# A new order for every step from the middle of the first feed-forward block on

## The chip, the cores and the metric

The kernel runs on one core of a Trainium2 chip. TensorE (PE in the profile) multiplies matrices, VectorE (DVE), ScalarE (ACT) and GpSimd (POOL) do the element-wise work, and SyncE (SP) issues the DMA transfers. Each engine works through its own list of instructions in the order in which the program wrote them, and waits on semaphores for the others. The metric is the device time of one execution in microseconds (us); a comparison uses the median over several executions.

## The reference

A Mamba-2 state-space layer on 4 batches of 8 heads, 768 positions, head width 32, state width 16, in chunks of 32, is followed by RMS norm and a SwiGLU feed-forward block. All is float32.

```python
for c in range(nc):                      # 24 chunks of 32 positions
    cum = np.cumsum(la, axis=-1)
    L = np.exp(cum[..., :, None] - cum[..., None, :]) * causal
    M = np.einsum('bhin,bhjn->bhij', Cc, Bc) * L
    y[:, :, sl] = np.einsum('bhij,bhjd->bhid', M, xc) + \
                  np.einsum('bhin,bhnd->bhid', Cc, state) * np.exp(cum)[..., None]
    state = decay_full * state + np.sum(Bx, axis=2)
# y is then read as (3072, 256)
xn = x / np.sqrt(np.mean(x * x, axis=-1, keepdims=True) + 1e-06) * rms_g
g = xn @ w_gate                          # (3072, 1536)
return (g * sigmoid(g) * (xn @ w_val)) @ w_out
```

## The kernel before

The 3072 tokens are worked in six blocks of 512. While TensorE multiplies for the feed-forward part of one block, the state-space layer of the next is prepared on the other engines.

**Gate and value.** Each block's two products with the 256 x 1536 weights are made by a Strassen-Winograd scheme: for each of six pairs `j` of 128-column groups, seven products `P.k.j` (`product_gv`, L951) stand for eight. Each is four matmul records of 128x256. Products 1, 4, 6 and 7 add up in a PSUM tile "gate", 2, 3 and 5 in a tile "val"; each of these two has two buffers. Step `take.k.j` copies a "gate" sum to SBUF as `p` (ScalarE, L957), `C.c.j` adds it to the "val" sum (VectorE, L963), `silu.c.j` is ScalarE's activation (L208), and `hid.c.j` (VectorE, `hidp` on GpSimd, L976) multiplies it with the value half into `hid`.

**Output.** Block 0 multiplies `hid` with `w_out` plainly (`o.f`, L983, eight records of 128x256 each). Blocks 1 to 5 use a 3x3 scheme with 20 products: `O.k.h` (`product_o`, L1072, four records of 128x128 for a half `h`), whose factors are sums of pieces of `hid` (`u.n` on VectorE and `up.n` on GpSimd, L1046) and sums of pieces of `w_out` (`two.n`, `twop.n`, L1028). `w.n` adds a product to the output tile `ob` (VectorE, L1103, or ScalarE, L1099 and L208), and `put.i` sends `ob` out (L1108). Ten of the products have no PSUM place of their own and reuse that of an earlier one (the table `SECOND`), so that such a product waits until the earlier one's last `w.n` has been done.

**State-space part and norm.** `spread` (L500, DMA), `sub` (L506) and `ex` (L208, L493) make the decay matrices `L`; `ex` needs another activation table on ScalarE than `silu`, and a table load stands before each change. `T`, `g` (L599), `L1` and `L` (L632), `y` (L736) and `S` (L688) follow. For the norm, `sq` squares, `ms` is a small matmul (L820), `rs` takes the roots on ScalarE and sends them to DRAM (L833), `rb` reads them back to all partitions (L838), `xn` scales (L847), and `tx` (L928) makes the differences that products 4 to 7 need.

**Weights.** In block 0 the weights arrive as raw integers (`fetch`) and are decoded by `pow` (ScalarE, two activations), `man` (VectorE, L224) and `wt` (VectorE, L230).

What sets the order is one string, `order` (from L1269), of 1667 steps. A loop (L1437) calls the function behind each name, block 0's from `first_kinds`, the others' from `kinds`, and each engine's own list is in the order of these calls. A name is block:kind.numbers, so `1:P.4.0` is product 4 of pair 0 in block 1.

Of the kernel before, what the change touches and what calls it, by code (L numbers as in the profile page):

```python
# [20 lines left out]
def kernel(  # L21
# [1217 lines left out]
    def of_chunk(n, fn):  # L1239
# [66 lines left out]
        1:P.2.1 1:C.11.1 0:man.16 1:P.6.1 1:take.6.1 1:P.5.0 1:P.6.0 1:take.6.0 1:P.7.1 1:P.5.1
        0:cwp.1.3 1:silu.11.1 0:wt.16 0:hidgp.22.5 0:sub.11 1:take.7.1 1:C.22.1 1:hid.11.1 0:ydone.3
        0:ex.9 1:P.7.0 0:man.17 1:take.7.0 1:P.4.1 1:P.3.1 1:P.4.0 1:C.22.0 1:silu.21.0 0:wt.17
        1:silu.22.1 1:silu.21.1 0:table.0 1:silu.22.0 1:hidp.22.0 1:dT.1 1:hid.21.0 1:P.3.0 1:cw.2.1
        1:spread.2 1:dT.0 0:o.6 1:spread.3 1:hid.21.1 1:twop.2 1:C.12.1 1:silu.11.0 1:two.3 1:P.1.3  # L1310
        1:take.1.3 1:cwp.2.2 1:hid.11.0 1:P.1.2 1:C.12.0 1:P.2.3 1:P.6.3 1:two.8 0:silug.12.4
        1:silu.12.1 1:hidp.12.1 1:take.1.2 0:hidg.12.4 1:take.6.3 1:sub.3 0:ex.10 1:P.6.2 1:two.0
        0:sq2.2.0.0 0:sq2.2.0.2 1:C.11.3 1:P.2.2 0:sq2.2.1.2 1:twop.1 1:twop.4 1:take.6.2 1:C.11.2
        1:P.7.3 0:sq2.2.1.3 0:ex.11 1:two.11 1:take.7.3 0:sq2.2.1.1 1:T.0.1 0:o.7 0:o.8 1:P.5.3
        1:ex.3 1:hidp.22.1 1:silu.12.0 0:sub.8 1:P.4.3 1:silu.21.3 1:silu.11.3 1:T.1.1 1:hid.12.0
        0:ex.8 1:P.7.2 1:two.5 1:two.10 1:hid.11.3 1:cwp.2.3 0:sq2.2.0.1 1:C.22.3 0:o.9 0:o.10
        0:o.11 1:P.5.2 1:P.3.3 1:silu.22.3 0:sq2.2.0.3 1:bc.0 1:scale2.0 1:take.7.2 1:Tt.0.1
        1:sq2.1.0 1:hid.21.3 1:subp.2 1:twop.7 1:spread.1 1:T.1.0 1:silu.11.2 1:Tt.0.0 1:bc.1
        1:P.4.2 1:silu.21.2 1:C.22.2 1:C.12.3 1:hidp.22.3 1:silu.12.3 1:hidp.12.3 1:x.0 1:subp.1
        1:hid.21.2 1:P.1.4 1:take.1.4 1:P.2.4 1:C.11.4 1:T.0.0 2:bc.0 1:P.3.2 1:Tt.1.1 1:P.6.4  # L1320
        2:bc.1 1:C.12.2 1:P.1.5 1:Tt.1.0 0:put.0 0:put.3 1:hid.11.2 1:P.2.5 1:Td.1 0:put.2
        1:take.6.4 0:put.1 1:take.1.5 1:C.11.5 1:silu.11.5 1:silu.12.2 1:scale2.1 1:hid.12.2 1:P.7.4
        1:P.6.5 1:take.7.4 1:silu.11.4 1:P.5.4 1:take.6.5 2:dT.0 1:P.4.4 1:silu.21.4 1:twop.6
        1:two.9 1:sq2.1.1 1:C.22.4 1:hid.11.5 1:sq2.0.0 1:g 1:hid.11.4 1:silu.22.4 1:Td.0 1:P.7.5
        1:hid.21.4 1:P.5.5 1:silu.22.2 1:L 1:sq2.1.2 1:O.2.0 1:L1.3 1:take.7.5 1:hidp.22.4 1:P.4.5
        1:C.22.5 1:L1.2 1:O.2.1 1:O.15.0 1:O.15.1 1:silu.22.5 1:u.0 1:hid.22.5 1:y.0 1:hid.22.2
        1:silu.21.5 1:w.0 1:hid.21.5 1:u.1 1:P.3.5 1:u.2 1:w.2 1:O.3.0 1:O.3.1 1:O.0.0 1:O.0.1 1:w.4
        1:P.3.4 1:O.17.0 1:C.12.5 1:silu.12.5 1:O.17.1 1:w.5 2:S.0 2:scale2.0 1:hid.12.5 1:w.10
        1:up.3 1:u.9 1:sq2.0.3 1:C.12.4 1:O.6.0 1:silu.12.4 1:O.6.1 0:exps 1:O.16.0 1:O.16.1
        1:sq2.1.3 1:w.1 2:T.1.1 2:Tt.1.1 1:x.1 1:up.4 1:up.5 1:hid.12.4 1:O.4.0 1:up.6 1:u.7  # L1330
        2:Tt.1.0 1:O.4.1 1:O.9.0 1:O.9.1 1:u.10 1:w.3 1:w.6 1:up.11 1:y.1 2:T.0.1 2:Tt.0.0 2:S.1
        1:O.18.0 1:O.18.1 1:sq 1:sq2.0.2 1:yt 1:O.8.0 1:w.11 1:u.8 1:w.12 1:sq2.0.1 1:w.8 1:O.8.1
        1:O.13.0 1:O.13.1 1:w.16 1:ms 1:rs 1:w.13 2:T.1.0 1:O.11.0 1:O.11.1 1:w.7 1:up.12 2:T.0.0
        3:bc.1 1:ex.1 1:O.5.0 1:O.5.1 1:w.20 1:O.12.0 1:O.12.1 2:Tt.0.1 1:O.7.0 1:O.7.1 1:up.13
        1:u.14 2:g 1:w.18 1:O.1.0 1:w.9 1:w.17 1:ex.2 1:O.1.1 1:w.15 1:w.14 1:O.14.0 1:O.14.1 2:Td.0
        1:u.15 1:O.19.0 1:O.19.1 1:w.22 1:w.19 1:rb 1:O.10.0 1:O.10.1 2:scale2.1 1:xn 1:w.24 1:tx.0
        1:txp.1 1:put.3 2:P.1.1 2:take.1.1 1:txp.2 2:spread.2 1:w.25 1:w.21 2:sq2.1.0 2:P.1.0
        1:sub.0 2:take.1.0 1:ex.0 2:P.2.1 2:C.11.1 2:silu.11.1 2:P.6.1 2:P.6.0 2:take.6.0 1:w.23
        2:P.5.1 2:L1.2 2:P.2.0 2:C.11.0 2:take.6.1 2:P.7.0 1:tx.3 2:take.7.0 2:P.7.1 2:take.7.1
        2:P.5.0 2:C.22.1 2:C.22.0 2:silu.22.1 2:P.4.0 2:silu.21.0 2:silu.11.0 2:P.4.1 2:spread.3  # L1340
        2:silu.21.1 2:silu.22.0 2:hid.11.1 2:P.3.1 2:L 2:P.3.0 2:hid.21.0 2:P.1.3 2:hidp.22.0
        2:hid.21.1 2:C.12.0 2:P.1.2 2:silu.12.0 2:hid.12.0 2:take.1.3 2:take.1.2 2:P.2.2 2:C.11.2
        1:put.0 2:L1.3 2:subp.3 2:P.6.3 2:dT.1 2:C.12.1 2:spread.1 2:silu.11.2 2:x.0 2:hid.11.2
        1:put.2 2:ex.3 2:P.6.2 2:take.6.2 3:dT.1 2:Td.1 2:take.6.3 2:hid.11.0 2:sq2.0.0 2:y.0
        2:P.2.3 2:C.11.3 2:sq2.1.2 2:silu.11.3 2:P.7.2 3:scale2.1 2:P.7.3 2:take.7.3 2:take.7.2
        2:subp.2 2:sub.1 2:silu.12.1 2:hidp.12.1 3:S.0 2:sq2.1.1 2:P.5.3 2:C.22.3 2:hid.22.1 2:x.1
        2:silu.22.3 2:hidp.22.3 2:P.5.2 2:C.22.2 2:sq2.1.3 2:P.4.3 2:y.1 3:S.1 2:sq 2:P.4.2
        2:silu.21.2 2:P.3.3 2:hid.21.2 2:C.12.3 2:silu.21.3 2:hid.21.3 2:hid.11.3 2:silu.12.3
        2:P.3.2 1:put.1 2:P.1.5 2:take.1.5 2:silu.22.2 3:T.1.1 3:Tt.1.1 2:C.12.2 2:hidp.12.3
        2:silu.12.2 2:P.1.4 2:sq2.0.3 2:hid.22.2 3:T.0.1 2:take.1.4 2:P.2.5 2:C.11.5 2:silu.11.5  # L1350
        2:hid.11.5 3:spread.0 3:Tt.0.0 2:P.6.5 2:take.6.5 2:P.6.4 2:take.6.4 2:P.2.4 2:C.11.4
        2:P.7.5 2:take.7.5 3:dT.0 2:P.7.4 2:spread.0 2:subp.0 3:Tt.1.0 3:Td.1 2:take.7.4 2:sq2.0.1
        2:P.5.4 2:C.22.4 2:silu.11.4 2:yt 2:silu.22.4 3:subp.0 3:spread.3 2:P.4.5 2:P.4.4
        2:silu.21.4 2:P.5.5 2:ms 2:hid.11.4 2:hid.21.4 2:hidp.12.2 2:O.2.0 2:hidp.22.4 2:up.0
        2:O.2.1 2:O.15.0 2:silu.21.5 2:hid.21.5 2:C.22.5 2:O.15.1 3:exps 2:P.3.5 2:sq2.0.2
        3:spread.2 2:up.1 2:exps 2:u.3 2:up.4 2:rs 2:rb 3:T.1.0 3:T.0.0 2:ex.1 2:w.0 2:P.3.4 2:w.2
        2:O.3.0 2:C.12.5 2:C.12.4 3:sq2.1.0 2:silu.22.5 3:sq2.1.3 2:O.3.1 2:O.0.0 2:silu.12.5
        3:Tt.0.1 2:hid.12.5 2:O.6.0 2:O.6.1 2:O.16.0 2:O.16.1 2:w.1 2:hid.22.5 2:up.5 2:table
        2:O.0.1 3:spread.1 2:silu.12.4 3:g 2:w.4 2:u.2 2:xn 2:O.17.0 2:w.3 2:O.17.1 2:w.5 2:w.10
        3:P.1.0 3:P.2.0 2:hidp.12.4 2:u.9 2:txp.0 2:ex.0 2:tx.2 2:O.4.0 3:take.1.0 2:up.6 2:up.7  # L1360
        2:O.4.1 2:O.9.0 2:O.9.1 2:tx.1 2:tx.3 3:P.6.0 3:take.6.0 3:C.11.0 2:w.6 2:O.18.0 2:O.18.1
        2:w.11 2:w.12 2:w.7 2:w.13 3:P.5.0 2:w.8 2:w.9 2:ex.2 2:u.10 3:P.7.0 2:O.8.0 2:O.8.1
        2:O.13.0 2:O.13.1 2:w.16 3:P.1.1 2:O.5.0 2:O.5.1 3:take.7.0 3:C.22.0 3:silu.22.0 3:P.3.0
        2:up.8 3:take.1.1 3:P.6.1 3:take.6.1 3:P.4.0 3:silu.21.0 3:C.12.0 2:w.20 2:O.7.0 3:L1.3
        3:L1.2 3:sq2.1.2 2:up.11 2:up.12 3:subp.2 2:O.7.1 3:sub.3 3:sq2.0.0 3:silu.12.0 2:O.11.0
        2:O.11.1 3:sq2.0.1 2:O.12.0 2:up.13 2:O.12.1 2:w.17 2:w.15 3:P.7.1 3:take.7.1 2:w.18 2:w.14
        3:hid.21.0 2:u.14 3:table 2:O.1.0 2:O.1.1 2:w.22 3:silu.11.0 2:up.15 2:O.14.0 2:O.14.1
        2:O.19.0 2:O.19.1 3:P.4.1 3:silu.21.1 3:sq2.1.1 2:w.19 2:O.10.0 2:O.10.1 3:hid.22.0 2:w.23
        2:w.24 2:w.25 3:P.1.3 3:P.2.1 3:take.1.3 2:w.21 4:dT.0 3:Td.0 3:C.11.1 3:hid.21.1 3:x.0
        3:bc.0 3:P.2.3 3:subp.1 3:silu.11.1 2:put.3 3:scale2p.0 3:P.6.3 3:hid.12.0 3:hid.11.1  # L1370
# [108 lines left out]
```

## Time and profile before

| | |
|---|---|
| runs | 388.96, 389.95, 391.85 us; median 389.95 us |
| profiled execution | 389.76 us, of which the span from first to last instruction is 388.0 us |
| PE busy | 382.5 us, 99% of the span, 3805 records |
| DVE busy | 277.8 us, 72% |
| ACT busy | 214.3 us, 55%, with 22 table loads |
| POOL busy | 150.1 us, 39% |
| granted TensorE clock | 1.000 |

The profiled execution lies 0.19 us under the median. 1.76 us of it are outside the span. The span is what the views of the trace divide. Busy shares of matmuls overlap in their ends, so that how close TensorE stands to its pace is read from the time between starts, not from the busy time.

### The profile page before, as it was taken

What the parts mean: (1) busy time and instruction counts of PE and PEld (TensorE: products, weight loads), DVE (VectorE), ACT (ScalarE), POOL (GpSimd) and SP (SyncE); (2) the same over time, 40 slices, a digit from 0 to 9 for tenths busy, and PEclk for the clock granted to TensorE, in tenths of its full rate; (3) what the DMA queues carried; (4) which work ended last, traced back from release to release, by engine and by line L of the source; (5) the groups of instructions that cost most, each with busy time, mean ns of one, the idle gap of its engine ahead of it and who ended that gap; (6) DMA issues with size and microseconds to landing.
All of it is one profiled execution on the core that took longest, in us unless ns stands there. A gap on an engine that the chain in (4) does not pass through costs nothing.

```text
span 388.0 us, 9604 instructions
## 1 busy us (share of the span) xinstructions
PE 382.5 (99%) x3805; PEld 330.0 (85%) x3805; DVE 277.8 (72%) x593; ACT 214.3 (55%) x453; POOL 150.1 (39%) x168
## 2 busy tenths in 40 slices
...
PEclk9999999999999999999999999999999999999999
...
GB/s 91 236 128 233 311 169 179 124 166 30 3 101 87 52 11 96 144 42 100 65 75 85 27 42 42 2 18 19 56 3 2 2 14 48 29 1 0 2 0 56
DMA packets 109940, 28.04 MB, mean 72 GB/s; under 512 B 94824, under 2 KB 107848, under 8 KB 109896
## 3 DMA queue, kind: packets, MB, share of 16 engines
...
q14 instruction: 14, 0.11, 0.1%
...
## 4 chain that ended last, share of the span: by engine, by line
PE 97%; DVE 1%; ACT 1%; issue 0%; ACTq 0%; DVEq 0%
PE gate L951 29%; PE o L1072 23%; PE val L951 22%; PE o L983 5%; PE gate L865 4%; PE y L736 3%; PE gate L875 2%; PE g L599 2%; PE e L460 1%; PE g L592 1%; PE y L664 1%; PE tp L540 1%; PE e L474 0%; DVE ob L1103 0%; PE idle L328 0%
## 5 line engine op out<-in xcount | busy, mean ns | idle before, releaser
L963 DVE TENSOR_TENSOR c<-val,p 128x512 f32<-128x512 f32 x99 | 67.3, 686 | 49.4 <-PE val L951 35.2
L957 ACT COPY p<-gate 128x512 f32<-128x512 f32 x99 | 56.8, 581 | 61.6 <-PE gate L951 59.3
L951 PE MATMUL gate<-tx,wgv 128*128 128x256 f32 x264 | 65.8, 381 | 0.0
L208 ACT ACTIVATE c<-c 128x256 f32<-128x256 f32 x99 | 40.0, 415 | 39.2 <-DVE c L963 38.9
L976 POOL TENSOR_TENSOR hid<-c 128x256 f32<-128x256 f32 x31 | 23.8, 769 | 89.6 <-ACT c L208 84.9
L951 PEld LDWEIGHTS gate<-tx,wgv 128*128 128x128 f32 x264 | 49.3, 190 | 6.9 <-ACT p L957 0.2
L1103 DVE TENSOR_TENSOR ob<-ob,o 128x128 f32<-128x128 f32 (+1 forms) x90 | 24.2, 297 | 21.7 <-PE o L1072 16.9
L976 DVE TENSOR_TENSOR hid<-c 128x256 f32<-128x256 f32 x68 | 34.0, 513 | 6.7 <-ACT c L208 6.6
L1072 PE MATMUL o<-two,hid 128*128 128x128 f32 x280 | 36.5, 276 | 0.1
L1072 PEld LDWEIGHTS o<-two,hid 128*128 128x128 f32 x280 | 34.5, 192 | 1.1 <-DVE hid L976 0.4
L951 PE MATMUL val<-xn,wgv 128*128 128x256 f32 x132 | 33.7, 381 | 0.0
L951 PE MATMUL val<-tx,sw 128*128 128x256 f32 x132 | 33.5, 380 | 0.0
L951 PE MATMUL val<-xn,sw 128*128 128x256 f32 x132 | 33.3, 381 | 0.0
L951 PE MATMUL gate<-tx,sw 128*128 128x256 f32 x132 | 33.0, 380 | 0.0
L951 PE MATMUL gate<-xn,wgv 128*128 128x256 f32 x132 | 32.7, 380 | 0.0
L493 POOL TENSOR_SCALAR_AFFINE_SELECT L<-L 64x512 f32<-64x512 f32 x32 | 22.8, 713 | 18.1 <-ACT L L208 16.8
L951 PEld LDWEIGHTS val<-xn,wgv 128*128 128x128 f32 x132 | 24.8, 190 | 3.5
L951 PEld LDWEIGHTS val<-tx,sw 128*128 128x128 f32 x132 | 24.9, 190 | 3.4 <-issue 0.2
L951 PEld LDWEIGHTS gate<-tx,sw 128*128 128x128 f32 x132 | 24.8, 190 | 3.4 <-issue 0.2
L951 PEld LDWEIGHTS val<-xn,sw 128*128 128x128 f32 x132 | 24.4, 190 | 3.2 <-issue 0.2
L951 PEld LDWEIGHTS gate<-xn,wgv 128*128 128x128 f32 x132 | 24.4, 190 | 3.1
L208 ACT ACTIVATE u<-gate 128x256 f32<-128x256 f32 (+1 forms) x37 | 14.6, 402 | 18.2 <-PE gate L951 15.3
(202 smaller groups left out, 702.6 us busy)
## 6 DMA issues: line engine op xcount, KB each, us to landing
...
```

The source lines that it names most:

```text
L208: nc.scalar.activation(**operands)
L493: nc.gpsimd.affine_select(out=L[r], in_=L[r], pattern=[[0, L.shape[1]], [1, HC]], compare_op=ALU.is_ge, fill=0.0, base=0, channel_multipli ...
L599: nc.tensor.matmul(out=g[u, P * i:P * i + P].rearrange("p (t m) -> p t m", t=2), lhsT=T[r, i, 0, u], rhs=T[r, i, 1:3, u], start=(first and ...
L736: nc.tensor.matmul(out=y[2 * k + u][rows, (2 * n + i) * HC:(2 * n + i + 1) * HC], start=(k, u, rows.start) not in opened, stop=True, skip_ ...
L865: nc.tensor.matmul(out=gv[:, k], lhsT=w[:, t, fs], rhs=xns[0][:, t], start=(t == 0), stop=(t == 1))
L951: nc.tensor.matmul(out=dst[:, half[w]], lhsT=lhsT, rhs=rhs, start=(k in (1, 2, 5) and w == 0), stop=True, skip_group_check=True)
L957: nc.scalar.copy(out=t, in_=Xs[j])
L963: nc.vector.tensor_tensor(out=t, in0=Zs[j], in1=a, op=ALU.add)
L976: engine.tensor_tensor(out=hid[:, 2 * j + c // 10 - 1, c % 10 - 1], in0=u, in1=src[:, half[1]], op=ALU.mult)
L983: nc.tensor.matmul(out=o, lhsT=hid[:, f, k // 2, (k % 2) * P:(k % 2 + 1) * P], rhs=wo[:, f], start=opens, stop=(f == NF - 1), skip_group_c ...
L1072: nc.tensor.matmul(out=Os[blk, b][:, place * P:(place + 1) * P], lhsT=hidden_or_sum(u)[:, g], rhs=rhs, start=(blk, b) not in opened, stop= ...
L1103: nc.vector.tensor_tensor(out=o, in0=o, in1=src, op=ALU.add if what[0] == "+" else ALU.subtract)
```

## The change

Every step of the string after `0:P.3.5`, the third product of pair 5 in block 0, stands in a new order: 1333 of the 1667 steps, all but the first behind that product. The set of steps is the same. Each engine has as many instructions as before, except that ScalarE has 20 table loads and not 22, and that the waits between engines differ in number (TensorE 78 before and 74 now, VectorE 188 and 182, ScalarE 96 and 103, GpSimd 69 and 57, SyncE 72 and 78). The order is one that was fitted with a little time added to every hand-over between two engines. Since the first `put` of block 0 is now number 1, the allocation of its output tile asks whether the tile is there, and not for number 0.

```diff
     def put(k):
-        if k == 0:
+        if 0 not in obs:
             obs[0] = ffn.tile([P, 2, 2, DM], FP32, tag="ob", name="ob", bufs=1)
...
-        0:cw.1.1 0:o.2 0:o.3 0:silug.21.5 0:hidg.21.5 1:spread.0 0:cwp.5.3 0:P.3.5 0:pow.14 0:man.14
-        0:wt.14 0:o.4 0:rb.1 0:pow.15 0:sq2.2.1.0 0:fetch.16 0:hidg.11.5 0:pow.17 0:C.12.5 0:C.12.4
...
+        0:cw.1.1 0:o.2 0:o.3 0:silug.21.5 0:hidg.21.5 1:spread.0 0:cwp.5.3 0:P.3.5 0:pow.14
+        0:silug.22.5 0:pow.15 0:cwp.1.3 0:C.12.4 0:silug.12.4 0:pow.17 0:rb.1 1:dT.0 0:sq2.2.1.3
...
-        5:up.13 5:w.14 5:w.9 5:O.12.1 5:w.17 5:w.18 5:w.15 5:put.3 5:u.14 5:O.1.0 5:O.1.1 5:w.19
...
+        5:w.20 5:w.15 5:w.14 5:w.16 5:O.12.0 5:O.12.1 5:O.11.0 5:O.11.1 5:u.14 5:w.22 5:w.18 5:O.5.0
+        5:O.14.0 5:O.5.1 5:w.17 5:put.3 5:u.15 5:O.1.0 5:O.1.1 5:w.19 5:O.19.0 5:O.14.1 5:O.19.1
...
```

**First place: VectorE ahead of block 1's first product.** These rows of VectorE start at the last product of block 0's pair 5, `hid<-u,gate`. `m` and `wo` are the decoding of `w_out`, `c` the sums `C`, `xn` the scaled input of block 1, which its first product on TensorE waits for, and `L<-L,tok` is `0:sub.11`. Before:

```order
L976 TENSOR_TENSOR hid<-u,gate 128x256
L224 TENSOR_SCALAR m<-wr 128x512
L230 TENSOR_TENSOR wo<-m,e 128x512
L976 TENSOR_TENSOR hid<-c 128x256
L963 TENSOR_TENSOR c<-val,p 128x512 x2
L847 SCALAR_TENSOR_TENSOR xn<-yt,gcol,sq 128x512 x2
L928 TENSOR_TENSOR tx<-xn 128x256 x2
```

Now:

```order
L976 TENSOR_TENSOR hid<-u,gate 128x256
L963 TENSOR_TENSOR c<-val,p 128x512
L976 TENSOR_TENSOR hid<-c 128x256
L224 TENSOR_SCALAR m<-wr 128x512 x2
L230 TENSOR_TENSOR wo<-m,e 128x512
L506 TENSOR_TENSOR L<-L,tok 128x512
L224 TENSOR_SCALAR m<-wr 128x512
L847 SCALAR_TENSOR_TENSOR xn<-yt,gcol,sq 128x512 x2
L963 TENSOR_TENSOR c<-val,p 128x512
```

Two more `m` and the `L` stand ahead of `xn`, and one `c` has gone behind it. On TensorE the product `0:o.5`, which stood ahead of block 1's first product, stands behind `1:P.6.0` now, so `xn` is wanted one such product (eight records) earlier.

**Second place: ScalarE ahead of `take.7.0` of block 1.** These rows of ScalarE end at the copies `take.7.0` and `take.7.1` (`p<-gate`); `c` is a `silu`, `L` an `ex`, and product `1:P.4.0` of TensorE waits for `take.7.0`. Before, from `take.6.1` on:

```order
L957 COPY p<-gate 128x512 x2
L208 ACTIVATE c<-c 128x256
L957 COPY p<-gate 128x512
L202 ACT_TABLE_LOAD
L208 ACTIVATE L<-L 128x512
L957 COPY p<-gate 128x512
```

Now, from `take.6.1` on:

```order
L957 COPY p<-gate 128x512
L208 ACTIVATE c<-c 128x256
L957 COPY p<-gate 128x512
L208 ACTIVATE c<-c 128x256
L202 ACT_TABLE_LOAD
L208 ACTIVATE L<-L 128x512
L208 ACTIVATE L<-L 128x512
L208 ACTIVATE L<-L 128x512
L957 COPY p<-gate 128x512
L957 COPY p<-gate 128x512
```

Three `ex` stand together behind one table load and ahead of `take.7.0`, where one stood between two copies.

**Third place: TensorE at the end of block 5.** These rows are the last products `O` of the program up to its last matmul. `5:O.12` is `o<-two,hid` on the factor `a21`; `o<-sw,hid` and `o<-sw_793,hid` are the two halves of `5:O.1`, which takes the PSUM place of `5:O.11` and waits for that product's last sum, `w.18`, on VectorE; `o<-wo,s` is `5:O.14` and the last row `5:O.10`. Before:

```order
L1072 MATMUL o<-two,hid 128x128 x6
L1072 MATMUL o<-two,s 128x128 x4
L1072 MATMUL o<-two,hid 128x128 x2
L1072 MATMUL o<-sw,hid 128x128 x2
L1072 MATMUL o<-sw_793,hid 128x128 x2
L1072 MATMUL o<-wo,s 128x128 x4
L1072 MATMUL o<-two,hid 128x128 x4
L1072 MATMUL o<-wo,hid 128x128 x4
```

Now:

```order
L1072 MATMUL o<-two,s 128x128 x4
L1072 MATMUL o<-two,hid 128x128 x2
L1072 MATMUL o<-wo,s 128x128 x2
L1072 MATMUL o<-two,hid 128x128 x2
L1072 MATMUL o<-sw,hid 128x128 x2
L1072 MATMUL o<-sw_793,hid 128x128 x2
L1072 MATMUL o<-two,hid 128x128 x2
L1072 MATMUL o<-wo,s 128x128 x2
L1072 MATMUL o<-two,hid 128x128 x2
L1072 MATMUL o<-wo,hid 128x128 x4
```

Before, `5:O.12.1` (`o<-two,hid`, two matmuls) stands directly ahead of `5:O.1.0`. Now three halves, `5:O.5.0`, `5:O.14.0` and `5:O.5.1`, stand between the four matmuls of `5:O.11` (`o<-two,s`) and `5:O.1.0`, and `5:O.12` stands ahead of them all.

More of the change, by code (lines that the diff above doesn't have):

```diff
@@ L1306 @@
[L1306 to L1370, printed above, removed]
-        3:P.1.4 3:C.11.3 3:L 3:P.5.1 3:P.5.3 3:hid.11.0 3:take.6.3 3:silu.11.3 3:hid.11.3 3:take.1.4
@@ new lines @@
+        1:ex.3 0:ex.10 0:sub.8 1:cw.2.1 1:cwp.2.3 1:P.7.0 0:ex.11 1:take.7.0 1:P.5.0 1:C.22.0
+        1:P.7.1 1:P.5.1 1:P.4.0 1:take.7.1 1:twop.1 0:sq2.2.0.3 0:sq2.2.1.1 0:sq2.2.1.2 1:C.22.1
+        1:T.1.1 1:T.0.1 1:P.4.1 1:silu.22.0 1:Tt.1.0 1:silu.21.1 1:bc.1 1:spread.1 1:bc.0
+        1:silu.21.0 0:sq2.2.0.2 1:dT.1 1:hid.21.1 1:hid.21.0 1:P.3.1 1:C.12.1 1:silu.12.1
+        1:hidp.12.1 1:cwp.2.2 1:P.3.0 1:P.1.3 1:take.1.3 1:two.0 1:hid.11.0 1:C.12.0 1:subp.1 0:ex.9
+        1:Tt.0.0 1:Tt.0.1 0:ex.8 1:hidp.22.0 1:twop.7 1:P.2.3 1:C.11.3 0:o.6 1:two.3 1:P.1.2
@@ new lines @@
+        1:take.1.2 1:P.6.3 1:P.2.2 1:C.11.2 1:take.6.3 1:silu.11.3 1:Tt.1.1 1:silu.11.2 0:o.7 0:o.8
+        1:P.6.2 1:scale2.0 1:two.8 1:Td.1 1:take.6.2 1:P.7.3 1:P.5.3 1:two.5 1:hid.11.2 0:sq2.2.0.1
+        1:T.0.0 0:o.9 0:o.10 1:P.7.2 0:ydone.3 1:take.7.3 1:two.10 1:two.11 1:C.22.3 1:silu.22.1
+        1:hid.11.3 1:silu.22.3 1:take.7.2 1:x.0 1:sq2.1.0 2:bc.1 2:bc.0 1:T.1.0 1:P.3.3 1:C.12.3
+        0:o.11 1:hidp.22.3 1:spread.2 1:subp.2 1:twop.4 1:hidp.22.1 1:silu.12.0 0:put.1 0:put.2
+        0:put.3 0:put.0 1:P.4.3 1:silu.21.3 1:P.5.2 1:P.4.2 1:hid.12.0 1:hid.21.3 1:P.1.4 1:C.22.2
@@ new lines @@
+        1:P.2.5 1:silu.12.3 1:silu.21.2 1:take.1.4 1:hid.21.2 1:P.3.2 1:C.12.2 1:hidp.12.3 1:P.6.4
+        1:take.6.4 1:P.1.5 1:take.1.5 0:table.0 1:C.11.5 1:P.2.4 1:silu.11.5 1:C.11.4 1:silu.12.2
+        1:scale2.1 1:hid.12.2 1:P.7.4 1:P.6.5 1:take.7.4 1:silu.11.4 1:sq2.1.1 1:sq2.0.3 1:sq2.1.2
+        2:dT.1 1:P.5.4 1:sq2.0.2 3:bc.1 1:take.6.5 1:two.9 1:Td.0 1:P.4.4 1:hid.11.4 1:sq2.0.0
+        1:C.22.4 1:twop.6 1:silu.22.2 1:hid.22.2 1:sq2.0.1 2:dT.0 1:hid.11.5 1:sq2.1.3 1:g
+        1:silu.21.4 1:silu.22.4 1:hid.21.4 1:hidp.22.4 1:P.7.5 1:O.15.0 1:P.5.5 1:L1.3 1:L 1:L1.2
```

176 lines of the change are left out of this document (111 added, 65 removed).

## The prediction

> **What bounds the kernel now.** I read the page first, then the chain of waits that ended last, TensorE's waits, the engines' busy time by stretches, and at last the timeline at the places where the order changes.
>
> ```profile
> PE 382.5 (99%) x3805; PEld 330.0 (85%) x3805; DVE 277.8 (72%) x593; ACT 214.3 (55%) x453; POOL 150.1 (39%) x168
> PEclk9999999999999999999999999999999999999999
> PE 97%; DVE 1%; ACT 1%; issue 0%; ACTq 0%; DVEq 0%
> ```
>
> TensorE is busy for 99% of the span, the chain that ended last is 97% TensorE, and its granted clock is full in every slice. What it waits for is short:
>
> ```profile
> PE idle L328 <- DVE warm L354: 1.1, 1, 1.1
> PE y L705 <- DVE S L686: 0.5, 1, 0.5
> PE o L1072 <- DVE ob L1103: 0.4, 1, 0.4
> ```
>
> The first of these is at the start, ahead of the change. The stretches and the chain's rows say whether the busy time is dense:
>
> ```profile
> 78.00:88.00 10.00, 10.00 (x48) 8.81 (x47) 7.82 (x16) 5.00 (x9) 0.73 (x1) 1.00 0.85 162
> 88.00:98.00 10.00, 10.00 (x48) 8.81 (x47) 6.59 (x12) 7.66 (x15) 4.38 (x5) 1.00 0.26 26
> 77.80:381.00 303.20, 302.71 (x2893) 272.65 (x2891) 210.22 (x430) 157.03 (x347) 124.13 (x127) 1.00 0.23 44
> ...
> 78.81 3.45 PE o L983 x16
> 327.16 1.73 PE gate L951 x8
> 328.89 1.78 PE o L1072 x16
> ```
>
> A row of a stretch has TensorE's busy time with the records in brackets, then the weight loads, VectorE, ScalarE, GpSimd. 48 records of 128x256 in 10 us are 208 ns each. The chain's rows give the pace where nothing intervenes: 1.73/8 = 216 ns for such a record, so 0.86 us for a product `P` and 1.73 us for `o.f`, and 1.78/16 = 111 ns for a 128x128 record, 0.445 us for a half `O`. The changed part starts at 77.8 us. In the 303.2 us from there to 381, TensorE is without a matmul for 0.5 us. A new order of the same matmuls can therefore save about 0.5 us of idle time and some tenths in entries to short groups, not several us.
>
> The page "Perfetto Trace Analysis" of the Trainium skill (section "Identifying the Most-Contended Engine") warns that matmul busy time is no good measure of TensorE's headroom and wants the share of weight loads; that is 85% here, which would leave 15%. The start-to-start rows above do not bear that room out, and the rival on the fast side below prices it.
>
> **The change part by part.** The sum is made against the profiled execution, 389.76 us (span 388.0 and 1.76 around it), 0.19 under the median of 389.95. All operations stay, so only waits can change the end.
>
> *What it removes: the stall at the end.*
>
> ```profile
> 380.24 1.06 DVE L1103 TENSOR_TENSOR ob<-ob,o 128x128 f32<-128x128 f32 x4 [1.31 <-PE o L1072]
> 380.38 0.28 PE L1072 MATMUL o<-two,hid 128*128 128x128 f32 x1
> 381.03 1.16 PE L1072 MATMUL o<-sw,hid 128*128 128x128 f32 x8 [0.38 <-DVE ob L1103]
> 384.01 1.21 DVE L1103 TENSOR_TENSOR ob<-ob,o 128x128 f32<-128x128 f32 x4 [0.70 <-PE o L1072]
> ```
>
> The last record of `5:O.12.1` starts at 380.38, the first of `5:O.1.0` at 381.03: 0.65 us where 0.11 is the pace, so 0.54 us lost. `5:O.1.0` wants the place that `w.18` empties, and `w.18` stands among four `w` that start only behind `5:O.12.1`. In the new order three halves stand between `5:O.11` and `5:O.1.0`, 3 x 0.445 = 1.34 us of cover. VectorE needs ahead of `w.18` one sum `u` and one `w` more, by the rows for these 0.68 and 0.28, then 0.28 for itself: 1.24 from the end of `5:O.12`, which lies another 0.89 us earlier. So the stall goes: 0.54, and 0.1 for smaller gaps ahead of it; I take -0.65. The bounds are 0, if something else is late there, and -1.0, if every gap of this block end goes. Behind the last product the same row at 384.01 remains, with the last transfers, so nothing changes there.
>
> *What it adds: VectorE's list ahead of block 1's first product.*
>
> ```profile
> 74.95 0.42 DVE L976 TENSOR_TENSOR hid<-u,gate 128x256 f32<-128x256 f32 x1 [0.41 <-ACT u L208]
> 75.29 0.81 DVE L224 TENSOR_SCALAR m<-wr 128x512 int32<-128x512 uint32 x1
> 80.13 1.41 DVE L847 SCALAR_TENSOR_TENSOR xn<-yt,gcol,sq 128x512 f32<-128x512 f32 x2
> 81.45 0.75 DVE L928 TENSOR_TENSOR tx<-xn 128x256 f32<-128x256 f32 x2
> 85.94 0.68 DVE L963 TENSOR_TENSOR c<-val,p 128x512 f32<-128x512 f32 x1
> 86.55 0.41 DVE L224 TENSOR_SCALAR m<-wr 128x512 int32<-128x512 uint32 x1
> 87.06 0.69 DVE L230 TENSOR_TENSOR wo<-m,e 128x512 int32<-128x512 int32 x1
> 87.67 0.68 DVE L506 TENSOR_TENSOR L<-L,tok 128x512 f32<-128x512 f32 x1
> ```
>
> Start to start these are 0.34 for `hid`, 0.61 for `c`, `wo` and `L`, 0.4 for `m`, 1.32 for the two `xn`. The new list from 74.95: two `hid` 0.68, `c` 0.61, three `m` 1.2, `wo` 0.61, `L` 0.61, `xn` 1.32, in sum 5.0, so `xn` is whole at 80.0; with the 0.81 that `m` took here beside GpSimd's work, and a stretched `wo`, at 80.5. TensorE wants it when `o.4` has ended: it starts at about 78.65 and ends at 80.38, where `o.5` covered until 82.10 before. Product 1 needs only the first half of `xn`. So the price lies between 0 and 0.8; nearest to the first row of that kind I take +0.2. Behind it `wo`, the `tx` and `C.11` wait in VectorE's list, each with 0.5 us or more until its product.
>
> *ScalarE ahead of `1:P.4.0`.*
>
> ```profile
> 88.35 0.58 ACT L957 COPY p<-gate 128x512 f32<-128x512 f32 x1 [1.14 <-PE gate L951]
> 100.17 1.28 ACT L202 ACT_TABLE_LOAD   x1
> 101.47 0.63 ACT L208 ACTIVATE L<-L 128x512 f32<-128x512 f32 x1
> 102.00 0.57 ACT L957 COPY p<-gate 128x512 f32<-128x512 f32 x1
> ```
>
> By TensorE's pace `1:P.6.0` ends at 85.56; its copy can end at 86.4, a `silu` (0.35) at 86.75, the table load at 88.05, three `ex` of 0.53 at 89.65, `take.7.0` at 90.2. `1:P.4.0` is due at 80.38 plus six products, `o.5`, and four more, 90.74, and needs the copy some 0.2 us before. The slack is 0.3 us, and an `ex` waits for an `L<-L,tok` and a transfer besides. Bounds 0 and 0.6; I take +0.2.
>
> *The end of block 1.*
>
> ```profile
> 123.80 0.69 DVE L963 TENSOR_TENSOR c<-val,p 128x512 f32<-128x512 f32 x1
> 124.41 0.75 DVE L976 TENSOR_TENSOR hid<-c 128x256 f32<-128x256 f32 x2
> 125.41 0.41 DVE L976 TENSOR_TENSOR hid<-u,gate 128x256 f32<-128x256 f32 x1
> 125.64 0.70 PE L951 MATMUL gate<-tx,wgv 128*128 128x256 f32 x2
> ```
>
> The `hid` at 125.41 feeds `1:O.15.0`. Before, four product steps stood between `1:P.7.5` (at 125.64) and it; now it follows `1:P.7.5` at once, due at 126.5, while another `hid` goes ahead on VectorE, so that it comes at 126.1 plus the hand-over of 0.2. Slack 0.2; bounds 0 and 0.5; I take +0.2. The many other hand-overs that get nearer or farther I cost at nothing: TensorE has two sums of each kind in PSUM, and they cover a delay of one product, 0.86 us; without that cover each would cost up to its delay.
>
> The sum: 389.76 - 0.65 + 0.2 + 0.2 + 0.2 = 389.7 us.
>
> **The rivals.** *VectorE and GpSimd crowd each other (slower).*
>
> ```profile
> 130.65 0.69 DVE L1046 TENSOR_TENSOR s<-hid 128x512 f32<-128x512 f32 x1
> 130.69 1.77 POOL L1046 TENSOR_TENSOR hid<-hid 128x512 f32<-128x512 f32 x1 [4.59 <-DVE hid L976]
> 131.37 1.64 DVE L1046 TENSOR_TENSOR hid<-hid 128x512 f32<-128x512 f32 x1
> 380.35 1.27 POOL L1046 TENSOR_TENSOR s<-s,hid 128x512 f32<-128x512 f32 x1 [5.49 <-PE o L1072]
> ```
>
> One sum takes VectorE 0.69 us and, beside GpSimd's, 1.64; GpSimd's 1.27 become 1.77. The section "SBUF: two separate sides" of "SBUF — State Buffer" in the Trainium skill calls the two engines' shared port pair an exclusive lock, where the later instruction waits for the whole of the other; the row at 131.37 agrees, 0.95 us late, though the one at 130.65 ran beside GpSimd unharmed. The new order lists, ahead of the matmuls due between 78 and 88 us, 14.4 us of VectorE work (before 8.9) and 7.2 of GpSimd's (0.7), and in the next 10 us 11.0 of GpSimd's (6.1), each instruction at the time it took before. If VectorE is stretched by 30%, it is 14.4 x 0.3 = 4.3 us later; that decides once it exceeds the slack of 0.5 us at block 1's first products. Then about 389.7 + 4.3 = 394.0. Against it: work that is listed early need not be wanted early, and of the 14.4 us some 4 (`L`, `wo`, a `hid`) have no matmul waiting within 5 us.
>
> *The roots come late.*
>
> ```profile
> 193.74 0.36 SPq L833 DMA_DIRECT2D roots<-r  x1
> 195.94 1.74 SPq L838 DMA_DIRECT2D sq<-roots  x4
> 197.78 3.04 SPq L133 DMA_DIRECT2D squares<-in_C_dram  x4
> ```
>
> The norm of block 2 has its way to DRAM and back, issue to issue 2.2 us. SyncE issues one transfer in about 0.5 us (four in 1.74), and the new order puts ten of the squares' transfers ahead of the roots and two behind them. If SyncE is held at these, the ten cost up to 5 us, but the new order also leaves three us more of matmuls between `ms` and block 3's first product: about 2 us late, 391.7 us, within 1%.
>
> *TensorE gains pace (faster).* If matmuls could follow each other as fast as their weights load, the 303.2 us would be 272.65, and the time 359. Against it: the 208 ns between records stand whether VectorE and ScalarE are busy for 16 instructions or 12. To be faster by 1%, 385.9 us or less, the order would have to win 3.9 us, eight times the idle time found.
>
> **How the numbers follow.** Forecast, small stalls traded for one: 0.70. Roots late: 0.10. Crowding: 0.17, since the new order leaves more hand-overs on thin slack than I have priced. Faster by pace: 0.03. A measurement of this kernel can tell about 1% from no change; the runs before spread from 388.96 to 391.85. Predicted 389.7 us. The range reaches down by the bound of the stall and the runs' scatter (389.7 - 0.6 - 1.0, about 388.1) and up over the three prices at their bounds (0.8 + 0.6 + 0.5 in place of 0.6, 391.0) and the late roots to part of the crowding, 393.2. Faster by over 1%: 0.03; within 1%, the forecast and the late roots: 0.80; slower: 0.17.
>
> **What would show it.** Right: TensorE's 0.4 us wait for `ob` gone, 48 records in each 10 us from 78 on, and no wait of TensorE above 0.5 us. The gap ahead of block 1's first product shows the second term, one at 90.7 the third, one ahead of `1:O.15.0` the fourth. Wrong: fewer than 46 records in a stretch from 78 to 118 with VectorE above 9 us busy (crowding), or TensorE waiting for `xn` at block 3's start (roots).

## The result: 388.9 us against 389.5, no difference that is clear of the scatter

Over 22 runs each, the changed kernel takes 388.9 us at the median (387.86 to 392.33) and the kernel before 389.5 (388.56 to 392.66): a ratio of 0.9986 with a 95% interval from 0.9971 to 1.0002. The profiled execution took 389.11 us with a span of 387.3, where before it was 389.76 with 388.0. The page after:

```profile
PE 381.6 (99%) x3805; PEld 328.9 (85%) x3805; DVE 268.5 (69%) x593; ACT 213.6 (55%) x451; POOL 149.9 (39%) x168
PE 94%; DVE 2%; DMA 2%; issue 1%; ACT 0%; SPq 0%; DVEq 0%
```

TensorE is as full as before. VectorE is busy for 9.3 us less with the same 593 instructions; which kinds became shorter is said further down. TensorE's waits after:

```profile
PE idle L328 <- DVE warm L354: 1.1, 1, 1.1
PE g L599 <- DVE T L573: 0.7, 1, 0.7
PE y L705 <- DVE S L686: 0.3, 1, 0.3
```

The wait for `ob` is gone, and the wait of `g` for `T` belongs to the start, ahead of the change. In the stretches (TensorE's busy time and records, weight loads, VectorE, ScalarE, GpSimd) there are again 48 records in 10 us (46 or 47 that start there, and those that reach over the edges):

```profile
78.00:88.00 10.00, 10.00 (x48) 8.81 (x47) 9.97 (x21) 7.86 (x14) 2.59 (x2) 1.00 0.80 140
88.00:98.00 10.00, 10.00 (x48) 8.81 (x47) 7.72 (x14) 8.42 (x16) 9.29 (x12) 1.00 0.74 96
77.80:380.50 302.70, 302.50 (x2891) 272.08 (x2890) 201.07 (x429) 155.87 (x344) 124.67 (x127) 1.00 0.23 44
```

**An account in place of the waits.** TensorE's waits list only three idle spells, and small gaps hide under overlapping ends. So I took the start of each product from the trace and compared the time to the next start with the pace (0.863 us for `P`, 0.445 for a half `O`, 1.727 for `o.f`, the same group's own time before for `g`, `y` and `ms`). The account runs from the first record of `0:P.3.5` to the first of `5:O.10.1`, the last product. The first start is in these rows, of the kernel before and of the changed kernel:

```profile
77.79 1.03 PE L951 MATMUL val<-xn,sw 128*128 128x256 f32 x4
```

```profile
77.33 1.03 PE L951 MATMUL val<-xn,sw 128*128 128x256 f32 x4
```

| us | before | changed |
|---|---|---|
| start of `0:P.3.5` | 77.79 | 77.33 |
| from there to `5:O.10.1` | 306.47 | 306.30 |
| of it above the pace | 4.10 | 3.93 |
| of that in steps of about 0.1 us | 3.22 in 33 places | 3.24 in 33 places |

Of the 0.63 us by which the last product is earlier, 0.46 lie ahead of the first changed step, in instructions that are the same: in the profiles of eleven kernels of this study that are the same up to there, the start of `0:P.3.5` lies anywhere from 76.53 to 78.43. The changed order itself wins 0.17 us. It gains the stall at the end and loses most of that again in new gaps. (Taking a small group's time before as its pace hides one gain: from `2:ms` to the next product it is 0.56 us before, where that product waits for a `hid`, and 0.36 after.) The end of block 5 after:

```profile
380.50 0.61 PE L1072 MATMUL o<-two,hid 128*128 128x128 f32 x4
380.95 1.06 PE L1072 MATMUL o<-sw,hid 128*128 128x128 f32 x8
383.38 1.18 DVE L1103 TENSOR_TENSOR ob<-ob,o 128x256 f32<-128x256 f32 x4 [1.05 <-PE o L1072]
```

From `5:O.5.1` at 380.50 to `5:O.1.0` at 380.95 it is the pace. The new gaps are in three places:

```profile
135.99 1.27 POOL L1046 TENSOR_TENSOR s<-s,hid 128x512 f32<-128x512 f32 x1
136.27 1.53 DVE L1046 TENSOR_TENSOR s<-s,hid 128x512 f32<-128x512 f32 x1
137.85 0.97 PEld L1072 LDWEIGHTS o<-sw,s 128*128 128x128 f32 x8 [0.32 <-DVE s L1046]
...
153.34 0.73 PEld L951 LDWEIGHTS gate<-xn,wgv 128*128 128x128 f32 x4 [0.20 <-DVE xn L847]
...
251.26 1.27 POOL L1046 TENSOR_TENSOR s<-hid 128x512 f32<-128x512 f32 x1 [5.60 <-DVE hid L976]
251.28 1.79 DVE L1046 TENSOR_TENSOR hid<-hid 128x512 f32<-128x512 f32 x1
253.00 0.68 DVE L963 TENSOR_TENSOR c<-val,p 128x512 f32<-128x512 f32 x1
253.73 0.73 PEld L951 LDWEIGHTS val<-xn,sw 128*128 128x128 f32 x4 [0.25 <-DVE c L963]
```

`1:u.9` took 1.53 us on VectorE instead of 0.69, and `1:O.9.0` came 0.30 late. `3:u.3` took 1.79, so that `3:C.22.2` behind it, and with it `3:P.3.2`, came 0.22 late. `3:ms` came 0.20 late, where 0.10 is usual ahead of such a group (its entry, priced below). The other 0.10 is a step that follows nearly every pause of TensorE in these accounts: 0.10 also stands behind `1:O.9.0` and `2:P.1.1`. At `1:u.9` and `3:u.3` alike, VectorE's sum began just behind one of GpSimd's and ended 0.54 us after GpSimd's end (137.26 and 137.80, 252.53 and 253.07). `2:P.1.1` waited 0.17 for `xn`.

### The profile page after: what moved, and what is told of

The parts are those of the page before. It is cut to its first block, busy times and chain, and to the rows that moved or that the text cites. A ratio compares the mean times of both kernels' runs of the same rounds, so it can differ in the third digit from the quotient of the medians.

```text
span 387.3 us, 9593 instructions
## 1 busy us (share of the span) xinstructions
PE 381.6 (99%) x3805; PEld 328.9 (85%) x3805; DVE 268.5 (69%) x593; ACT 213.6 (55%) x451; POOL 149.9 (39%) x168
## 4 chain that ended last, share of the span: by engine, by line
PE 94%; DVE 2%; DMA 2%; issue 1%; ACT 0%; SPq 0%; DVEq 0%
PE gate L951 30%; PE o L1072 23%; PE val L951 22%; PE o L983 5%; PE y L736 3%; PE gate L865 3%; PE g L599 2%; DMA rowe<-e_sb 1%; PE e L460 1%; DMA dT<-rowe 1%; PE gate L875 1%; PE g L592 1%; PE y L664 1%; PE tp L540 1%; PE e L474 0%
## 5 line engine op out<-in xcount | busy, mean ns | idle before, releaser
L976 POOL TENSOR_TENSOR hid<-c 128x256 f32<-128x256 f32 x31 | 24.3, 785 | 94.1 <-ACT c L208 87.5
L1072 PE MATMUL o<-two,hid 128*128 128x128 f32 x280 | 38.7, 275 | 0.0
L1072 PEld LDWEIGHTS o<-two,hid 128*128 128x128 f32 x280 | 35.6, 192 | 0.7 <-issue 0.2
L976 DVE TENSOR_TENSOR hid<-c 128x256 f32<-128x256 f32 x68 | 30.6, 460 | 7.2 <-ACT c L208 6.8
L1046 POOL TENSOR_TENSOR s<-hid 128x512 f32<-128x512 f32 x13 | 17.3, 1330 | 22.6 <-DVE hid L976 16.2
```

Of the source, the lines that this page charges most:

```text
L976: engine.tensor_tensor(out=hid[:, 2 * j + c // 10 - 1, c % 10 - 1], in0=u, in1=src[:, half[1]], op=ALU.mult)
L1046: engine.tensor_tensor(out=hidden_or_sum(o), in0=hidden_or_sum(in0), in1=hidden_or_sum(in1), op=ALU.add if in1[0] == "+" else ALU.subtract)
L1072: nc.tensor.matmul(out=Os[blk, b][:, place * P:(place + 1) * P], lhsT=hidden_or_sum(u)[:, g], rhs=rhs, start=(blk, b) not in opened, stop= ...
```

## The experiments

Ratios are to the kernel before, of runs on the same chip, with their 95% intervals; the time from `0:P.3.5` to `5:O.10.1` is called the stretch. Each title has the name of its kernel in brackets.

**Cover for the stall, by a product that was not ready** (tail_only).

```diff
-5:u.14 5:O.1.0 5:O.1.1 5:w.19 5:put.0 5:O.14.0 5:u.15 5:w.22 5:O.14.1
+5:u.14 5:O.14.0 5:O.14.1 5:O.1.0 5:O.1.1 5:w.19 5:put.0 5:u.15 5:w.22
```

> The kernel before with one move: both halves of 5:O.14 go ahead of 5:O.1.0, so that 0.89 us of products stand between the last half of 5:O.12 and 5:O.1.0, which waits for w.18. My theory (the stall at the end adds to the time one to one): the gap of 0.65 us ahead of 5:O.1.0 falls to 0.11 to 0.2 and the last product ends 0.4 to 0.55 us earlier relative to the start of 0:P.3.5; the median is 0.1 to 0.14% lower. Rival (the sums on VectorE behind it, not the products, set the end): the gap closes and the end stays where it was.

Measured: 390.29 us, 1.0036 (1.0023 to 1.0049), slower. The stall did not close:

```profile
380.22 1.27 POOL L1046 TENSOR_TENSOR s<-s,hid 128x512 f32<-128x512 f32 x1 [5.50 <-PE o L1072]
381.54 1.16 PE L1072 MATMUL o<-wo,s 128*128 128x128 f32 x8 [1.02 <-POOL s L1046]
```

`5:O.14` multiplies by a sum that GpSimd makes until 381.49, so TensorE waited 1.19 us there, and 0.45 ahead of `5:O.10.0` later. The stretch is 308.34, 1.87 above before: 0.65 more than the old 0.54 ahead of `5:O.14.0`, 0.45 ahead of `5:O.10.0`, 0.44 ahead of `3:P.1.0`, where the roots came late in this execution, and 0.33 in smaller steps. Both theories had it wrong, since neither asked whether the cover itself was ready.

**The wait alone, moved forward** (w18_early).

```diff
-5:w.8 5:w.16 5:O.5.0 5:w.13 5:w.7 5:O.5.1 ... 5:O.12.1 5:w.17 5:w.18 5:w.15
+5:w.8 5:w.16 5:O.5.0 5:w.13 5:w.18 5:w.7 5:O.5.1 ... 5:O.12.1 5:w.17 5:w.15
```

> The kernel before with one move: 5:w.18 goes from behind 5:O.12.1 to behind 5:w.13 on VectorE, some 2 us earlier, and no product moves. My theory (the stall at the end was the wait of w.18 behind products of the same PSUM bank, nothing else): the gap of 0.65 us ahead of 5:O.1.0 falls to 0.11, the last product comes 0.5 to 0.6 us earlier from the start of 0:P.3.5, and the median is 0.13 to 0.16% lower; in tail_only the stall went over to 5:O.14, whose factor GpSimd had not finished, so it had been only moved. Rival (another late operand stands behind w.18): a gap of 0.3 us or more stays ahead of 5:O.1.0 or comes ahead of 5:O.14.0 and 5:O.10.0.

Measured: 388.85 us, 1.0002 (0.9991 to 1.0013), the same; stretch 306.51. The rival was right that another late operand stands behind, though the largest gap came ahead of `5:O.12.0`, which it did not name:

```profile
379.53 0.71 PE L1072 MATMUL o<-two,hid 128*128 128x128 f32 x4 [0.29 <-DVE hid L1046]
380.97 0.61 PE L1072 MATMUL o<-two,hid 128*128 128x128 f32 x4
381.42 1.06 PE L1072 MATMUL o<-sw,hid 128*128 128x128 f32 x8
382.60 1.16 PE L1072 MATMUL o<-wo,s 128*128 128x128 f32 x8
```

`5:O.1.0` at 381.42 follows at the pace, but 0.45 us now stand ahead of `5:O.12.0` (0.19 stood behind it before) and 0.29 ahead of `5:O.14.0`. The old end of block 5 is a net of hand-overs that are all tight; one wait taken out of it goes to the next.

**The changed order without its cover** (no_cover).

```diff
-5:w.18 5:O.5.0 5:O.14.0 5:O.5.1 5:w.17 5:put.3 5:u.15 5:O.1.0 5:O.1.1
+5:w.18 5:w.17 5:put.3 5:u.15 5:O.1.0 5:O.1.1 5:O.5.0 5:O.14.0 5:O.5.1
```

> The changed kernel with the three halves 5:O.5.0, 5:O.14.0 and 5:O.5.1 moved behind 5:O.1.1, so that nothing stands between 5:O.11.1 and 5:O.1.0. My theory: a stall of 0.5 to 0.9 us comes back ahead of 5:O.1.0 (w.18 stands behind u.14 and w.22 on VectorE), and the time grows by as much, 0.13 to 0.23% over the changed kernel, back to that of the kernel before or above. Rival (that stall was not what separates the two kernels): the time stays at that of the changed kernel.

In this kernel `5:w.17` stands ahead of the product `5:O.5` that it should add, so it adds what lay in that place. Measured: 389.51 us, 1.0016 (1.0005 to 1.0027).

```profile
380.86 1.16 PE L1072 MATMUL o<-sw,hid 128*128 128x128 f32 x8 [0.70 <-DVE ob L1103]
```

The account has 0.87 us ahead of `5:O.1.0`, as expected. The stretch grew by 1.91 to 308.21; nearly all the rest, 0.95, is at `2:P.1.1`, 1.12 late in this execution and 0.17 in the changed kernel's. Only the 0.87 and the step of 0.10 behind it belong to the edit. By the two ratios (1.0016 and 0.9986) the time grew by 0.3%, more than the 0.13 to 0.23% expected; that the wait at `2:P.1.1` fills the rest in the other runs too is not shown.

**VectorE and GpSimd kept apart** (meet_less).

```diff
-1:hid.12.5 1:O.16.0 ... 1:w.10 1:u.9 1:O.4.1
+1:hid.12.5 1:u.9 1:O.16.0 ... 1:w.10 1:O.4.1
-3:hid.21.2 3:u.3 3:up.1 3:up.2 3:up.4 3:yt 3:P.5.2 3:C.22.2 3:O.15.0
+3:hid.21.2 3:P.5.2 3:C.22.2 3:u.3 3:up.1 3:up.2 3:up.4 3:yt 3:O.15.0
```

> The changed kernel with two moves on VectorE: 1:u.9 goes to right behind 1:hid.12.5, ahead of GpSimd's up.5, and 3:C.22.2 (with 3:P.5.2) ahead of 3:u.3. My theory (a VectorE instruction with two SBUF inputs stands still while GpSimd works, which made u.9 1.53 us and u.3 1.79 us instead of 0.69, and so TensorE's gaps of 0.30 us ahead of 1:O.9.0 and 0.22 and 0.10 us ahead of 3:P.3.2 and 3:ms): u.9 takes 0.69, both gaps go, the last product ends 0.4 to 0.6 us earlier from the start of 0:P.3.5. Rival (these products are late for another reason, as the copies on ScalarE): the gaps stay or move by less than 0.1 us.

Measured: 388.29 us, 0.9977 (0.9966 to 0.9989), faster than before; from the changed kernel the runs do not part it, since the two intervals overlap. `1:u.9` and GpSimd's next sum:

```profile
133.74 0.69 DVE L1046 TENSOR_TENSOR s<-s,hid 128x512 f32<-128x512 f32 x1
134.00 1.56 POOL L1046 TENSOR_TENSOR s<-hid 128x512 f32<-128x512 f32 x1 [1.75 <-DVE hid L976]
```

Now VectorE begins first and keeps its 0.69; GpSimd's sum, 0.26 us later, takes 1.56 and not 1.27. The gaps aimed at are gone, and ahead of `3:ms` only its entry of 0.10 is left. The stretch is 305.10, 1.20 less than the changed kernel's. Of these, 0.72 belong to the gaps aimed at (0.30 and 0.22, and a step of 0.10 behind each). The rest, 0.48, the edit did not aim at: this execution had neither the wait of 0.17 at `2:P.1.1` nor three steps of 0.10 in block 2 (in `2:P.1.1`, `2:P.7.1` and `2:P.5.0`).

**The roots first** (roots_first).

```diff
-2:spread.1 2:sq2.1.0 1:w.16 ... 2:x.0 1:rb 1:xn
+2:spread.1 1:w.16 ... 1:rb 2:x.0 2:sq2.1.0 1:xn
```

> The changed kernel with SyncE's four transfers of 2:sq2.1.0 (squares) and two of 2:x.0 moved behind the read-back of the roots, 1:rb. My theory (the roots of block 2's norm stood behind those squares on SyncE, 2.0 us from 143.97 to 145.97, which made xn late): the roots go out about 1 us earlier, the gap of 0.17 us between 1:O.10.1 and 2:P.1.1 goes, time lower by 0.1 to 0.2 us, less than can be told from the runs alone. Rival (the roots' trip through DRAM sets it, whatever stands ahead): the gap stays.

Measured: 388.35 us, 0.998 (0.997 to 0.9991); stretch 305.84. SyncE in the changed kernel, and then here:

```profile
143.97 2.00 SPq L133 DMA_DIRECT2D squares<-in_C_dram  x4
146.06 0.39 SPq L833 DMA_DIRECT2D roots<-r  x1
...
147.73 1.90 SPq L838 DMA_DIRECT2D sq<-roots  x4
```

```profile
145.98 0.35 SPq L833 DMA_DIRECT2D roots<-r  x1
147.76 1.76 SPq L838 DMA_DIRECT2D sq<-roots  x4
```

The two executions start 0.51 us apart at `0:P.3.5`, so the roots go out 0.59 us earlier here, not the full 1. No gap stands at `2:P.1.1`, and the three steps of 0.10 in block 2 are gone too; together these are the 0.46 us by which the stretch is shorter. With SyncE's old order the gap was 0.17, 1.12, 0 and 0.98 us in four executions (the changed kernel, no_cover, meet_less, xn_late) and 0 in after_pad; with the new order it was 0 in roots_first, both_moves, beside_g and y_apart. That the order of transfers took it away is likely, not shown, since two executions of the old one had no gap either.

**Both together** (both_moves). The edits are those of the last two.

> The changed kernel with the moves of meet_less and of roots_first together. My theory (TensorE's gaps add to the time one to one, and what is left is the pace and the entries to short groups): from the start of 0:P.3.5 to the last product 305.0 to 305.3 us, where the changed kernel took 306.30 and the kernel before 306.47; no gap over 0.12 us; the median 0.25 to 0.4% under the kernel before. Rival (the runs scatter in the transfers, and the fixes only shift which product waits): 305.8 or more, and no lower than meet_less or roots_first alone.

Measured: 387.59 us, 0.9962 (0.9949 to 0.9976), which is 0.4% under the kernel before and, by the two ratios, whose intervals just overlap, 0.2% under the changed kernel; stretch 305.10, no gap over 0.12. The stretch is that of meet_less, so the roots' part shows only where the transfers are slow. Its ratio is the lowest of those measured here.

**Slack ahead of block 1, tried** (xn_late).

```diff
-0:xn.1 1:P.1.0 1:take.1.0 1:P.1.1 0:C.12.5 0:wt.15 0:hidg.12.4
+0:C.12.5 0:wt.15 0:hidg.12.4 0:xn.1 1:P.1.0 1:take.1.0 1:P.1.1
```

> The changed kernel with 0:C.12.5, 0:wt.15 and 0:hidg.12.4 moved ahead of 0:xn.1 on VectorE, 0.61 + 0.61 + 0.34 = 1.56 us. In the changed kernel's trace the first half of xn was ready some 0.7 us before 1:P.1.0. Theory of slack (a hand-over costs only what exceeds its slack): a gap of 0.8 to 1.1 us ahead of 1:P.1.0. The prediction's way of pricing (a part of the delay, whatever the slack): 0.2 to 0.4. If something else covers it, as PSUM's two sums: none.

One execution, 390.05 us.

```profile
79.22 1.40 DVE L847 SCALAR_TENSOR_TENSOR xn<-yt,gcol,sq 128x512 f32<-128x512 f32 x2
80.02 1.99 PE L951 MATMUL gate<-xn,wgv 128*128 128x256 f32 x8 [0.73 <-DVE xn L847]
```

The account has 0.89 us ahead of `1:P.1.0`: 1.56 of delay less some 0.7 of slack. What exceeds the slack is paid whole, and a step of 0.10 follows in the next product.

**The same delay for both orders** (before_pad, after_pad).

```diff
 def total_gv(blk, c, j):
+    for _ in range(3):
+        nc.vector.memset(pad, 0.0)
```

> The kernel before with three VectorE writes of zeros to a spare 128x32 tile ahead of each of the 99 C sums (L963), perhaps 0.2 us each time and 20 us in all, on an engine that is busy for 72%. It tells how much slack the order leaves at VectorE's hand-overs. Theory (the new order, fitted with time added to every hand-over, has more slack): the kernel before grows by 4 to 8 us with it, the changed kernel by half of that or less. Rival (slack at the tight places is the same): both grow alike, within 1 us.

> The changed kernel with the same three VectorE writes ahead of each C sum. Theory (more slack in the new order): it grows by half or less of what the kernel before grows by. Rival (the slack is the same): alike, within 1 us.

```profile
L964 DVE MEMSET pad<- 128x32 f32 x297 | 25.2, 85 | 14.5
```

Measured: the kernel before grows to 394.03 us, 1.0105 (1.0055 to 1.0155), the changed one to 391.38, 1.0041 (1.0024 to 1.0059). From 1 and from 0.9986 these are 4.1 and 2.1 us. In the stretch it is 3.82 (306.47 to 310.29) and 1.23 (306.30 to 307.53). So the new order has more slack at VectorE's hand-overs: it grows by a half to a third as much. The factor is rough, since the interval of the kernel before is wide and each stretch is one execution. That is what fitting it with time added to hand-overs would give; in the undisturbed kernel it is worth almost nothing, because the old order's slack was nearly enough.

**The price of an entry** (beside_g, then y_apart). Some 30 steps of 0.09 to 0.10 us remain in every account, one in front of each of 15 groups of small tiles (`g`, `y`, `ms`; two neighbours count as one) and one a product behind it. In the first try two `g` went beside `ms`:

```diff
-2:ms 2:rs ... 3:exps 3:g 3:x.0
+2:ms 3:g 2:rs ... 3:exps 3:x.0
-3:ms 3:rs ... 4:silu.22.0 4:g 4:P.4.1
+3:ms 4:g 3:rs ... 4:silu.22.0 4:P.4.1
```

> both_moves, and two groups g (L599) moved to right behind the norm's small matmuls: 3:g behind 2:ms and 4:g behind 3:ms. My theory (each change between full-size products and the groups of small tiles costs TensorE 0.09 us on the way in and 0.10 in one of the next products, so that two neighbouring groups pay once): two entries less, 0.35 to 0.45 us less than both_moves from 0:P.3.5 to the last product, 0.1% of the time. Rival (the 0.2 us belongs to each group's own first and last matmuls, beside what they stand is the same): no difference, within 0.05 us in the trace.

Measured: 393.68 us, 1.0123 (1.0106 to 1.014).

```profile
PE g L599 <- ACT r L208: 3.2, 2, 2.6
258.09 1.61 PE L599 MATMUL g<-T 32*64 32x128 f32 x52 [2.63 <-ACT r L208]
260.00:262.00 2.00, 2.00 (x11) 2.00 (x11) 0.00 (x0) 0.00 (x0) 0.00 (x0) 0.52 0.24 68
262.00:264.00 2.00, 2.00 (x20) 2.00 (x20) 0.97 (x2) 0.28 (x1) 0.65 (x1) 1.00 0.22 63
```

`g` now waited for ScalarE, which makes the roots from `ms` (stretch 311.55). The first row is of TensorE's waits, the second of the timeline, the last two are stretches, where the third number from the end is the granted clock. Behind the wait of 2.63 us ahead of `4:g` TensorE's clock was 0.52 of the full one for the next products: 11 records in 2 us instead of 20. So a long pause cost more than itself here; the pause of 1.19 us in tail_only left the clock at 1.00. On the entries this try says nothing. The second try goes the other way and parts the two `y` of block 4 by one move in both_moves:

```diff
-4:y.0 4:y.1 4:P.7.2
+4:y.0 4:P.7.2 4:y.1
```

> both_moves with one move: 4:y.1 goes behind 4:P.7.2, so that the two groups y of block 4, neighbours until now, have a full-size product between them. Theory of entries (each change from full-size products to a group of small tiles costs TensorE 0.09 us, and one of the products behind it 0.10 more): 0.19 to 0.21 us more from 0:P.3.5 to the last product, 305.3 against 305.10, seen as 0.09 ahead of 4:y.1 and 0.10 behind it. Rival (the cost belongs to each group itself and was paid by both neighbours already): 305.1.

One execution, 387.9 us; TensorE in both_moves and then here:

```profile
288.03 0.49 PE L736 MATMUL y<-T,S 32*64 32x64 f32 x32
288.45 0.86 PE L736 MATMUL y<-L,xr 64*32 64x64 f32 x64
289.24 0.49 PE L736 MATMUL y<-T,S 32*64 32x64 f32 x32
```

```profile
289.09 0.86 PE L736 MATMUL y<-L,xr 64*32 64x64 f32 x64
289.88 1.13 PE L951 MATMUL gate<-tx,wgv 128*128 128x256 f32 x4
290.94 0.49 PE L736 MATMUL y<-T,S 32*64 32x64 f32 x32
```

The stretch is 305.32, 0.22 above both_moves: from 289.88 to 290.94 it is 1.06 us for a product of 0.86. An entry costs TensorE about 0.2 us, and neighbouring groups share it. The rival is out, as far as one execution of each can tell. The half behind the group is not peculiar to small tiles: the same 0.10 stands behind stalls with no group near, as behind `5:O.1.0` before (0.54 late) and `1:P.1.0` above (0.89 late).

## Why the prediction held, and where its steps did not

**The bound: right in kind, too low in size.** TensorE's pace sets the time, and the order moved the stretch by 0.17 of 306 us, where a sum of -0.05 was forecast. But what an order can win was put at 0.5 us and some tenths; the account has 4.1 us above the pace, and both_moves, on top of the new order, took the stretch 1.37 under the kernel before. The pace in the stretches was also read too short: 48 records in 10 us are not 208 ns each, since those that reach over the edges count too; starts lie 216 ns apart before and after, as the chain's rows say.

**The stall at the end: right as a term, incomplete as a reason.** It was to give 0.65, and the account of the changed kernel has none of the 0.54 and 0.19 there. no_cover brings 0.87 back when the three halves go, so they are the cover. But the two edits of the old order show that moving the cover or the wait alone gains nothing: the new order also has each factor and each place ready in time.

**The three prices at VectorE and ScalarE: wrong, all at their lower bound of 0.** The same three hand-overs after:

```profile
78.45 1.40 DVE L847 SCALAR_TENSOR_TENSOR xn<-yt,gcol,sq 128x512 f32<-128x512 f32 x2
79.92 1.89 PE L951 MATMUL gate<-xn,wgv 128*128 128x256 f32 x8
...
89.09 1.17 ACT L957 COPY p<-gate 128x512 f32<-128x512 f32 x2
90.28 1.89 PE L951 MATMUL gate<-tx,wgv 128*128 128x256 f32 x8
...
124.97 0.42 DVE L976 TENSOR_TENSOR hid<-u,gate 128x256 f32<-128x256 f32 x1
126.14 0.61 PE L1072 MATMUL o<-two,hid 128*128 128x128 f32 x4
```

The first half of `xn` is done 0.7 us ahead of its product, `take.7.0` 0.6, the `hid` 0.75. The step that failed is that a slack of some tenths was given a price of some tenths; xn_late shows that a hand-over costs everything beyond its slack, and these three that it costs nothing up to it. The hand-over of 0.2 that two of the sums added was too long at least for VectorE: in the kernel with the late `xn` its first half ends at 79.96 and the product starts at 80.02. The sum of durations for `xn` was near: whole 0.07 us ahead of its use, where 0.4 before to 0.1 after had been worked out.

**What came instead:** gaps of 0.30, 0.17, 0.22 and 0.10 us in places that were not priced, 0.8 in sum, close to the 0.6 of the three that were. The total was right by two errors that met: that is luck, and the runs could not have told the forecast from no change.

**Crowding, the slower rival: its cause is real, its price was wrong.** VectorE was full in its stretch, 9.97 of 10 us, and nothing waited. The price took every VectorE instruction as 30% longer. The groups of the page say which are; first before, then after:

```profile
L963 DVE TENSOR_TENSOR c<-val,p 128x512 f32<-128x512 f32 x99 | 67.3, 686 | 49.4 <-PE val L951 35.2
L976 DVE TENSOR_TENSOR hid<-c 128x256 f32<-128x256 f32 x68 | 34.0, 513 | 6.7 <-ACT c L208 6.6
```

```profile
L963 DVE TENSOR_TENSOR c<-val,p 128x512 f32<-128x512 f32 x99 | 67.3, 688 | 57.5 <-PE val L951 32.7
L976 DVE TENSOR_TENSOR hid<-c 128x256 f32<-128x256 f32 x68 | 30.6, 460 | 7.2 <-ACT c L208 6.8
```

The sums `C`, which TensorE waits for most, read one input from PSUM and take 0.69 us whatever GpSimd does: in the changed part before, 52 of them ran alone and 40 beside an instruction of GpSimd for at least 5% of their time, at 688 and 682 ns; after it is 689 and 687. Those with two inputs in SBUF (`hid`, `u`, the `w_out` sums) are most of the ones that stretch: `hid` and the like (L976) 418 ns alone and 592 beside GpSimd before, 417 and 502 after. Added up one by one, all of VectorE's instructions take 8.4 us less than before (less than the 9.3 of busy time, which counts overlapping ends once), of which 3.6 are `hid` and the like, 1.9 the sums `u` and 1.7 the `w_out` sums.

**Roots late: it happened, at another block and smaller.** `xn` of block 2, not of block 3, came 0.17 late in the changed kernel and up to 1.12 in other executions of the same transfers, where about 2 us had been worked out. One part of the prediction must be read with care there: the step `2:rs`, which it called the norm of block 2, makes the input of block 3.

**Faster by pace: out.** 48 records in each 10 us as before.
